# Seven quarter products instead of eight in the second layer of a fused attention and maxout kernel

## The chip, the cores and the metric

The kernel runs on one core of a Trainium2 chip. The time is the device time of one launch in microseconds; the figure before is the median of three runs, 149.65 us (149.41 to 149.71). A profile is a record of one execution; its span runs from the first instruction to the last.

## The reference

For each of 8 batches and 8 heads, 512 tokens x (64 wide) read from 32 state rows, and the state rows read from the tokens, both by softmax attention. The heads are put side by side (512 wide), and a two-branch layer with a maximum follows:

```python
xread = softmax(scale * x @ state.T) @ state          # 512 rows of each batch
sread = softmax(scale * state @ x.T) @ x              # 32 rows of each batch
x = concat([xread, sread]) -> (8 * 544, 512)
h1, h2 = x @ w1, x @ w2                               # 512 -> 1024
out = maximum(h1, h2) @ w_out                         # 1024 -> 512
```

## The kernel before

**Arithmetic.** The matmuls take bf16 and sum in float32 in PSUM, which has eight banks of 128 x 512 floats. The maximum is written h2 + relu(h1 - h2). So wd holds w1 - w2, and wwo holds the product w2 w_out; the output is xread wwo + relu(xread wd) w_out. The attention of the tokens is folded into the weights too: for a batch, sw_s holds, for the 256 state rows of all heads in two groups of 128, their products with wd (columns 0 to FF = 1024) and with wwo (columns FF to WC = 1536). With at_s, the transposed attention weights (256 state rows by 512 tokens), the first layer is r = relu(at_s x sw_s), transposed, 8 tiles of 128 features by 512 tokens (r_s, `l1_mm`, two matmuls a tile, evicted by `l1_ev` on ScalarE and VectorE in turn). The second layer, `l2(b, c)`, makes one chunk of 128 tokens by 512 columns in one bank: two opening matmuls (`l2_open`, at_s by the wwo part of sw_s) and eight (`l2_f`, a 128-feature tile of r by the 512 columns of wo). `l2_out` copies the bank into an output buffer, on VectorE for even chunks and on ScalarE for odd ones.

**Order.** Each engine runs its instructions in the order in which the program issues them; semaphores order the engines among each other. A list of tokens written out by hand (`ORDER`) gives the weights' loading and batches 0 and 1, with the attention of batch 2. A loop over b = 2 to 6 then does, with n = b + 1: the casts and the DMA transpose of x of batch b + 2 (`cast_b` on GpSimd, `xt_dma`), the first layer of b, the scores of n (`sc_mm`) with their exponential on ScalarE (`sc_ev`), the sums over state rows and their reciprocals on VectorE (`red`), the product of both on GpSimd (`mul`), the DMA transpose to at_s (`at_dma`), the casts of x of b + 2 (`cast_e`, GpSimd), the load of x of b + 3, and then the four chunks of the second layer of b. Between chunks 1 and 2 stand sw of n (`sw_mm`, three pieces of two banks each, six copies by VectorE and ScalarE in turn) and sr of n (`sr_mm`, the state rows' reading, evicted by `sr_ev` on VectorE, transposed by `sr_tr` and copied by `sr_cp`). In the turns b = 2 and 3, `sr_ev` and `sr_tr` of batches 0 and 1 stand in the loop too, from a buffer in SBUF. Last comes the store of batch b. A part of its own after the loop does batch 7 with the state rows' rows (`m1`, `m2`) and stores in pieces.

**Banks.** `bank(ring)` deals out the banks of a ring in turn: ring "r" has six, for the first layer, scores, sw and transposes; ring "a" has two, for the second layer's chunks and sr. A matmul that opens a bank waits until the last copy out of it is done.

**Buffers.** Ten buffers `big` of 128 x 2048 floats hold the loaded x, the weights as loaded and the outputs, dealt out in rotation.

Of the kernel before, what the change touches and what calls it, by code (L numbers as in the profile page):

```python
# [41 lines left out]
l2.0.0.o@6 sc.2.0@1 l2.0.3.1@3 exp.2.0>A l2.1.1.3@0 l2.0.2.o@2 red.2.0>V l2.1.3.1@4 l2.1.3.0@4 srp.0>P srp.1>P  # L42
# [9 lines left out]
WHOLE = ()  # L52
# [5 lines left out]
def kernel(  # L58
# [40 lines left out]
    def copy(eng, o, i):  # L99
        if eng == "A":  # L100
            nc.scalar.copy(o, i)  # L101
        elif eng == "V":
            nc.vector.tensor_copy(o, i)  # L103
        else:
            nc.gpsimd.tensor_copy(o, i)  # L105
# [37 lines left out]


    slot = {}
    for k, key in enumerate(["x0", "w20", "w10", "wo0", "w21", "w11", "wo1", "x1", "x2", "x3", "o0", "x4", "o1", "x5",
                             "o2", "x6", "o3", "x7", "o4", "o5", "o6", "o7"]):
        slot[key] = big[k % 10]

    def xf(b):  # L150
        return slot[f"x{b}"].rearrange("p (h m) -> p h m", h=H)
# [1 line left out]
    def ob(b):  # L153
        return slot[f"o{b}"].rearrange("p (c n) -> p c n", c=NC)
# [217 lines left out]
    def l1_ev(p, b, f, eng=None):  # L372
        relu(r_s[b % 2][:, f, :], p, eng)
# [11 lines left out]
    def l2_out(b, c, p, eng, lo=0, hi=DM):  # L385
        copy(eng, ob(b)[:, c, lo:hi], p[:, lo:hi])

    def l2(b, c, eng=None, ring="a"):
# [2 lines left out]
        l2_f(b, c, p, range(NF), False, True)  # L391
        l2_out(b, c, p, eng or ("A" if c % 2 else "V"))

    def store(b, c0=0, c1=NC, lo=0, hi=DM, eng=None):
        dst = out[b * L:b * L + S].rearrange("(p c) n -> p c n", c=NC)
        (eng or nc.sync).dma_start(out=dst[:, c0:c1, lo:hi], in_=ob(b)[:, c0:c1, lo:hi])
# [114 lines left out]
    def sw_range(b, z):  # L511
# [13 lines left out]
        idle=idle, fill=lambda k, r: idle(1, r, 512 if k >= 100 else 256, k >= 200), cS=s_cast, mS=lambda z, e: s_mask(z, LATE, B, e), Sd=lambda: s_dma(LATE, B), ce=cast_e, cb=cast_b, xtd=xt_dma,  # L525
        atd=at_dma, red=lambda b, h, e: red(b, h), mul=mul, cw2=w2_cast, sub=w_sub, cwo=wo_cast, ww=ww_mm, l2=l2_mm,
        wwe=lambda i, e: copy(e, wwo[:, i, :], open_[f"ww{i}"]), le=lambda b, c, e: l2_out(b, c, open_[f"l2{b}{c}"], e),
        Se=lambda lo, hi, j, e: s_ev(done[f"S.{lo}.{hi}"], lo, hi, j, e), store=store,
        swe=lambda b, z, g, e: sw_ev(done[f"sw.{b}.{z}"], b, *sw_range(b, z), g, e))
    done = {}  # L530
# [84 lines left out]

    for b in range(2, B - 1):
        n = b + 1
        if b + 2 < B:  # L620
            for g in range(2):
                cast_b(b + 2, g, "P")
            xt_dma(b + 2)
        for f in range(NF):
            l1_ev(l1_mm(b, f), b, f)
        pp = [sc_mm(n, hh) for hh in range(2)]
        for hh in range(2):
            sc_ev(pp[hh], n, hh)
        for hh in range(2):
            red(n, hh)  # L630
            mul(n, hh, "P")
        at_dma(n)
        if b + 2 < B:
            for k in range(4):
                cast_e(b + 2, k, "P")
        if b + 3 < B:
            if b + 3 in WHOLE:
                load_x(b + 3, 0, n=H)
            else:
                for g in range(2):  # L640
                    load_x(b + 3, g)
# [30 lines left out]
    l2(b, 0)  # L672
    l2(b, 1)
    store(b, 0, 2)
    tc.mark_branch_hint_location("gen", "LikelyTaken", [ENG.PE, ENG.Activation, ENG.DVE, ENG.Pool, ENG.SP])
    m2(0, "V")
    m_store(0)
    m2(1, "A")
    m_store(1)
    l2(b, 2, "V")  # L680
    store(b, 2, 3)
    for z, (lo, hi) in enumerate(((0, 256), (256, 512))):
        p = bank("a")
        l2_open(b, 3, p, True, False, lo, hi)
        l2_f(b, 3, p, range(NF), False, True, lo, hi)
        l2_out(b, 3, p, "VA"[z], lo, hi)
        store(b, 3, 4, lo, hi)
# [35 lines left out]
```

## Time and profile before

| | |
|---|---|
| median of three runs | 149.65 us |
| the profiled execution: span from first to last instruction | 147.7 us |
| outside the span, against the median | 1.95 us |
| TensorE busy | 139.9 us (95%) |
| VectorE, ScalarE, GpSimd busy | 84.6 us (57%), 70.3 us (48%), 49.5 us (34%) |
| granted TensorE clock, mean | 0.997 |
| moved by DMA | 29.44 MB |

In the profile PE is TensorE, PEld its weight loads, DVE is VectorE, ACT is ScalarE, POOL is GpSimd and SP is SyncE, which issues the DMAs; a name ending in q is an engine's instruction queue. A group's line gives the source line, the engine, the operation, what it writes and reads, the shapes, the count, the busy time in us and the mean of one in ns, and then the idle time before it with what ended it. A timeline's line gives start and duration in us and how many instructions are merged in it. Matmuls overlap in the pipeline, so that the time between their starts, not their length, tells their pace. Many lines are those of helpers: L101, L103 and L105 are the copies on ScalarE, VectorE and GpSimd, whatever is copied; the names of the operands tell which.

### The profile page before, as it was taken

The numbers are of one execution on the slowest core, as the hardware profiler recorded it, in microseconds if no ns is written. First come the engines' busy times: TensorE is split into PE (matmuls) and PEld (weight loads), VectorE is DVE, ScalarE is ACT, GpSimd is POOL, SyncE is SP. The second block draws the span as 40 slices with busy tenths as digits, with TensorE's granted clock in tenths as the row PEclk, the third lists the DMA queues.
The fourth block names the chain that finished last, engine by engine and source line by source line (L and its number), as shares of the span: only waits on it lengthen the run. The fifth ranks groups of instructions, "written<-read, shape, count | busy, mean of one in ns | idle before, by whom it ended". The sixth has DMA issues, their size and how long they took to land.

```text
span 147.7 us, 3018 instructions
## 1 busy us (share of the span) xinstructions
PE 139.9 (95%) x1176; PEld 70.9 (48%) x1194; DVE 84.6 (57%) x162; ACT 70.3 (48%) x129; POOL 49.5 (34%) x85
## 2 busy tenths in 40 slices
PE   6988999999999999999999999999999999999990
PEld 3566725444454445444544444454445444854460
DVE  3488868773324838863884576275738586630130
ACT  4358789898031766246441835281546236511100
POOL 4156320295039900912590447227400500000000
PEclk9999999999999999999999999999999999999998
DMA  4999999939990759979989785787306033302232
GB/s 133 323 346 398 384 389 381 319 63 176 260 344 18 135 114 391 266 126 383 192 172 276 263 182 100 255 296 134 71 36 249 16 62 142 142 4 105 108 142 80
DMA packets 35807, 29.44 MB, mean 199 GB/s; under 512 B 22608, under 2 KB 31312, under 8 KB 34896
## 3 DMA queue, kind: packets, MB, share of 16 engines
q1 hardware_dynamic: 35520, 29.10, 67.4%
q8 instruction: 10, 0.16, 0.5%
q10 hardware_dynamic: 272, 0.13, 0.3%
q14 instruction: 5, 0.04, 0.1%
HBM read 15.20 MB, written 8.91 MB: 163 GB/s over the span
## 4 chain that ended last, share of the span: by engine, by line
PE 83%; DMA 11%; ACT 1%; issue 1%; DVE 0%; SPq 0%; DVEq 0%
PE bank L382 38%; PE bank L368 19%; PE bank L377 9%; DMA big<-in_moe_w_out_dram 8%; PE bank L345 4%; DMA big<-in_x_dram 3%; PE bank L502 3%; PE bank L401 2%; PE bank L411 2%; PE bank L257 2%; PE bank L297 1%; PE bank L409 1%; ACT wo L101 1%; PE bank L441 1%; DVE sw L103 0%
## 5 line engine op out<-in xcount | busy, mean ns | idle before, releaser
L382 PE MATMUL bank<-wo,r 128*128 128x512 bf16 (+1 forms) x259 | 60.6, 372 | 0.6 <-issue 0.2
L382 PEld LDWEIGHTS <-r 128*128 128x128 bf16 x264 | 25.5, 98 | 28.9 <-issue 0.5
L363 DVE TENSOR_SCALAR r<-bank 128x512 bf16<-128x512 f32 x32 | 21.8, 690 | 18.2 <-PE bank L368 17.7
L101 ACT COPY big<-bank 128x512 f32<-128x512 f32 (+1 forms) x16 | 9.2, 573 | 44.4 <-PE bank L382 39.7
L368 PE MATMUL bank<-at,sw 128*128 128x512 bf16 x127 | 29.7, 379 | 0.2 <-DVE sw L103 0.2
L273 POOL TENSOR_TENSOR a<-e,er 128x512 bf16<-128x512 bf16 x14 | 14.5, 1050 | 33.0 <-DVE er L270 23.4
L361 ACT ACTIVATE r<-bank 128x512 bf16<-128x512 f32 x32 | 19.4, 612 | 5.1 <-PE bank L368 4.8
L105 POOL CAST xb<-big 128x1024 bf16<-128x1024 f32 x12 | 12.4, 1043 | 21.5 <-issue 13.0
L368 PEld LDWEIGHTS <-sw 128*128 128x128 bf16 x128 | 12.2, 98 | 14.5 <-ACT sw L101 0.5
L103 DVE COPY big<-bank 128x512 f32<-128x512 f32 (+1 forms) x17 | 11.2, 661 | 13.0 <-PE bank L382 13.0
L103 DVE CAST sw<-bank 128x512 bf16<-128x512 f32 x23 | 14.5, 683 | 6.7 <-PE bank L345 6.7
L105 POOL CAST xe<-big 128x512 bf16<-128x512 f32 x27 | 16.1, 632 | 5.9 <-DMA big<-in_x_dram 5.9
L377 PE MATMUL bank<-sw,at 128*128 128x512 bf16 (+1 forms) x56 | 16.8, 372 | 0.3
L269 DVE TENSOR_REDUCE sums<-e 128x16 f32<-128x512 bf16 x16 | 10.7, 666 | 6.2 <-ACT e L265 6.2
L101 ACT CAST sw<-bank 128x512 bf16<-128x512 f32 x25 | 13.1, 600 | 1.4 <-PE bank L345 1.4
L265 ACT ACTIVATE e<-bank 128x512 bf16<-128x512 f32 x16 | 9.0, 595 | 6.3 <-PE bank L257 5.7
L468 PE MATMUL bank<-wz 128*128 128x256 bf16 (+1 forms) x26 | 7.2, 428 | 1.3 <-DVE ones L471 1.3
L377 PEld LDWEIGHTS <-at 128*128 128x128 bf16 x66 | 5.6, 98 | 5.0
L502 PE MATMUL bank<-wo,w2m 128*128 128x512 bf16 x31 | 7.7, 379 | 0.2 <-ACT wo L101 0.2
L257 PEld LDWEIGHTS <-xt 128*128 128x128 bf16 x128 | 5.1, 98 | 2.6 <-DVE sbd L103 0.7
L257 PE MATMUL bank<-sbd,xt 128*128 128x64 bf16 x128 | 5.5, 193 | 0.5 <-DVE sbd L103 0.5
L103 DVE COPY w2m<-bank 128x1024 bf16<-128x1024 bf16 (+1 forms) x5 | 3.3, 687 | 4.3 <-PE bank L411 4.1
(71 smaller groups left out, 111.5 us busy)
## 6 DMA issues: line engine op xcount, KB each, us to landing
big<-in_x_dram SPq DMA_DIRECT2D x16, 512.0 KB, 5.3
out_dram<-big SPq DMA_DIRECT2D x7, 1024.0 KB, 4.2
big<-in_moe_w_dram SPq DMA_DIRECT2D x8, 512.0 KB, 11.8
big<-in_moe_w_out_dram SPq DMA_DIRECT2D x4, 512.0 KB, 11.5
out_dram<-big SPq DMA_DIRECT2D x1, 512.0 KB, 2.6
out_dram<-w2m SPq DMA_DIRECT2D x2, 256.0 KB, 2.4
sf<-in_state_dram SPq DMA_DIRECT2D x1, 384.0 KB, 10.4
out_dram<-big SPq DMA_DIRECT2D x1, 256.0 KB, 2.7
```

The source lines that it names most:

```text
L101: nc.scalar.copy(o, i)
L103: nc.vector.tensor_copy(o, i)
L105: nc.gpsimd.tensor_copy(o, i)
L257: nc.tensor.matmul(pv[:, c, kk], xt_s[b % 2][:, c, k, :], sbd[:, b, k, :], start=(c == 0 and kk == 0), stop=(c == NC - 1 and kk == 1))
L269: nc.vector.tensor_reduce(es_all[:, b, hh], e_view(e_s[b % 2], hh), axis=AXX, op=ALU.add)
L273: (nc.gpsimd if eng == "P" else nc.vector).tensor_mul(e_view(a_s[b % 2], hh), e_view(e_s[b % 2], hh), er_s[b % 2][:, hh].unsqueeze(3).to_b ...
L361: nc.scalar.activation(out=o, in_=p, func=ACTF.Relu)
L363: nc.vector.tensor_scalar(o, p, scalar1=0.0, scalar2=None, op0=ALU.max)
L368: nc.tensor.matmul(p, sw_s[b % 3][:, g, f * 128:(f + 1) * 128], at_s[b % 3][:, g].rearrange("p c t -> p (c t)"), start=(g == 0), stop=(g = ...
L377: nc.tensor.matmul(p[:, lo:hi], at_s[b % 3][:, g, c, :], sw_s[b % 3][:, g, FF + lo:FF + hi], start=(start and g == 0), stop=(stop and g == 1))
L382: nc.tensor.matmul(p[:, lo:hi], r_s[b % 2][:, f, c * 128:(c + 1) * 128], wo[:, f, lo:hi], start=(start and j == 0), stop=(stop and j == le ...
L502: nc.tensor.matmul(p, w2t[:, f, i, :], wo[:, f, :], start=(first and f % 2 == 0), stop=(last and f % 2 == 1))
```

## The change

For batches 2 to 7 the second layer's product r wo (512 tokens by 1024 features by 512 columns) is cut into two by two by two quarters: tokens i, features j, columns k (`rq(b, i, j)`, `wq(j, k)`). By one level of Strassen's algorithm in Winograd's form the four output quarters come from seven products of quarters. Each product is 2 groups of 128 tokens by 4 feature tiles, 256 columns wide: eight matmuls.

- Sums of r quarters go into `st` (four for each batch: `r_sum` 0, 1 and 3 on VectorE, 2 on GpSimd), sums of wo quarters into `wt` (four in all, GpSimd, `w_sum`). All are bf16, 128 x 1024.
- Three fixed banks, BX, BY and BZ, hold the partial sums. Where a later product adds on top of an earlier partial sum, the bank stays, and `keep` copies the partial sum into `part` (float32 in SBUF) on ScalarE before. `put` writes an output quarter: on VectorE as the bank plus a kept sum, the last one as a ScalarE copy.
- The opening terms are added to three quarters in the bank (`opened`); the last quarter inherits the opening of another column half and gets the difference (`difference`, GpSimd, into `dif`).
- Ring "r" has five banks, the sixth is BZ, which sw's last piece also uses. sr takes its bank from ring "r" and no longer from "a". Of the six sw copies VectorE does two and ScalarE four.
- The buffers under `wt`, `st`, `part` and `dif` are those of the loaded wo halves and of half of w1, free by then; x5 to x7 and the outputs change to others (`HOME`).
- For batch 7, the seven products are interleaved with `m2`, and the first half's store is issued after the sixth product, right before the last two stores.

```diff
-l2.0.0.o@6 sc.2.0@1 ... red.2.0>V l2.1.3.1@4 l2.1.3.0@4 srp.0>P srp.1>P
+l2.0.0.o@6 sc.2.0@1 ... red.2.0>V l2.1.3.1@4 l2.1.3.0@4 srp.0>P srp.1>P wt.0>P wt.2>P wt.1>P
...
-    rings = {"r": RELEASE[0:6], "a": RELEASE[6:8]}
+    rings = {"r": RELEASE[0:5], "a": RELEASE[6:8]}
+    BZ, BX, BY = RELEASE[5:8]
...
+    def add(eng, o, i0, i1, op=ALU.add):
+        (nc.gpsimd if eng == "P" else nc.vector).tensor_tensor(o, i0, i1, op=op)
+    def wq(j, k):
+        return wo[:, 4 * j:4 * j + 4, 256 * k:256 * k + 256]
+    def rq(b, i, j):
+        return r_s[b % 2][:, 4 * j:4 * j + 4, 256 * i:256 * i + 256]
+    def w_sum(k, eng):
+        a, c = ((wq(0, 1), wq(0, 0)), (wq(1, 1), wt[:, 0]), (wq(1, 1), wq(0, 1)), (wq(1, 0), wt[:, 1]))[k]
+        add(eng, wt[:, k], a, c, ALU.subtract)
+    def r_sum(b, k, eng):
+        a, c, op = ((rq(b, 1, 0), rq(b, 1, 1), ALU.add), (st[:, 0], rq(b, 0, 0), ALU.subtract),
+                    (rq(b, 0, 0), rq(b, 1, 0), ALU.subtract), (rq(b, 0, 1), st[:, 1], ALU.subtract))[k]
+        add(eng, st[:, k], a, c, op)
+    def difference(b, eng):
+        s3 = sw_s[b % 3]
+        add(eng, dif[:, b % 2], s3[:, :, FF:FF + 256], s3[:, :, FF + 256:WC], ALU.subtract)
+    def product(pv, lhs, rhs, first=False, cc=(0, 1)):
+        for c in cc:
+            for f in range(4):
+                nc.tensor.matmul(pv[c], lhs[:, f, 128 * c:128 * c + 128], rhs[:, f, :],
+                                 start=first and f == 0 and (c == 0 or pv.split), stop=False, skip_group_check=True)
+    def opened(b, pv, i, rhs, cc=(0, 1)):
+        for c in cc:
+            for g in range(2):
+                nc.tensor.matmul(pv[c], at_s[b % 3][:, g, 2 * i + c, :], rhs[:, g, :], start=False, stop=False,
+                                 skip_group_check=True)
...
+    w_sum(3, "P")
+    difference(2, "P")
     for b in range(2, B - 1):
...
         for f in range(NF):
             l1_ev(l1_mm(b, f), b, f)
+        r_sum(b, 2, "P")
+        pX, pY, pZ = Pair(BX), Pair(BY), Pair(BZ)
+        product(pX, rq(b, 0, 0), wq(0, 0), True)
+        keep(0, pX, "A")
         pp = [sc_mm(n, hh) for hh in range(2)]
         for hh in range(2):
             sc_ev(pp[hh], n, hh)
+        r_sum(b, 0, "V")
+        r_sum(b, 1, "V")
+        product(pZ, rq(b, 0, 1), wq(1, 0), True)
+        opened(b, pZ, 0, so_half(b, 0))
         for hh in range(2):
             red(n, hh)
             mul(n, hh, "P")
...
-        l2(b, 0)
+        put(b, 0, 0, pZ, 0)
+        product(pX, st[:, 1], wt[:, 1])
+        keep(1, pX, "A")
+        product(pY, st[:, 0], wt[:, 0], True)
+        keep(2, pY, "A")
+        r_sum(b, 3, "V")
         if b < 4:
             sr_ev(srd[:, b - 2], b - 2)
-        l2(b, 1)
-        pg = [sw_mm(n, 512 * z, 512 * z + 512) for z in range(3)]
-        p = sr_mm(n, "a")
+        pg = [sw_mm(n, 512 * z, 512 * z + 512, "r", BZ if z == 2 else "r") for z in range(3)]
         for z in range(3):
             for g in range(2):
-                sw_ev(pg[z], n, 512 * z, 512 * z + 512, g, "VA"[(z + g) % 2])
+                sw_ev(pg[z], n, 512 * z, 512 * z + 512, g, "VAA"[(z + 2 * g) % 3])
+        difference(n, "P")
+        product(pX, st[:, 2], wt[:, 2])
+        opened(b, pX, 1, so_half(b, 1))
+        p = sr_mm(n, "r")
+        put(b, 1, 1, pX, 2)
         sr_ev(p, n)
-        l2(b, 2)
...
-        l2(b, 3)
+        product(pY, st[:, 3], wq(1, 1))
+        opened(b, pY, 0, so_half(b, 1))
+        put(b, 0, 1, pY, 1)
         sr_cp(sr_tr(n, "r"), n, "A")
+        product(pX, rq(b, 1, 1), wt[:, 3])
+        opened(b, pX, 1, dif[:, b % 2])
+        put(b, 1, 0, pX, None, "A")
```

More of the change, by code (lines that the diff above doesn't have):

```diff
@@ new lines, in opened, with __init__, __getitem__ @@
+    def opened(b, pv, i, rhs, cc=(0, 1)):
[3 more added lines that the diff above has]
+                                 skip_group_check=True)
+    class Pair:
+        def __init__(self, lo, hi=None):
+            self.split = hi is not None
+            self.p = [bank(lo)] + ([bank(hi)] if self.split else [])
+        def __getitem__(self, c):
+            return self.p[c][:, 0:256] if self.split else self.p[0][:, 256 * c:256 * c + 256]
@@ new lines, in out_q, with keep, put @@
+    def out_q(b, i, k):
+        return ob(b)[:, 2 * i:2 * i + 2, 256 * k:256 * k + 256]
+    def keep(k, pv, eng):
+        if pv.split:
+            for c in range(2):
+                copy(eng[c], part[:, k, 256 * c:256 * c + 256], pv[c])
+        else:
+            copy(eng, part[:, k], pv.p[0])
+    def put(b, i, k, pv, kept=None, eng="V"):
+        for c in ((0, 1) if pv.split else (None,)):
+            o = out_q(b, i, k) if c is None else out_q(b, i, k)[:, c]
+            p = pv.p[0].rearrange("p (c n) -> p c n", c=2) if c is None else pv[c]
+            if kept is None:
+                copy(eng, o, p)
+            else:
+                u = part[:, kept].rearrange("p (c n) -> p c n", c=2)
+                add("V", o, p, u if c is None else u[:, c])
@@ L671 @@
     fv = nc.values_load(flag[0:1, 0:1], skip_runtime_bounds_check_because="compared with zero alone")
-    l2(b, 0)
-    l2(b, 1)
-    store(b, 0, 2)
[L675 to L687, printed above, removed]
+    r_sum(b, 2, "P")
+    r_sum(b, 0, "V")
+    r_sum(b, 1, "V")
+    r_sum(b, 3, "V")
+    pX, pY, pZ = Pair(BX, "r"), Pair(BY), Pair(BZ)
+    product(pX, rq(b, 0, 0), wq(0, 0), True)
+    keep(0, pX, "AV")
+    product(pZ, rq(b, 0, 1), wq(1, 0), True)
+    opened(b, pZ, 0, so_half(b, 0))
+    put(b, 0, 0, pZ, 0)
+    product(pX, st[:, 1], wt[:, 1])
+    keep(1, pX, "AV")
+    product(pY, st[:, 0], wt[:, 0], True)
+    keep(2, pY, "A")
+    tc.mark_branch_hint_location("gen", "LikelyTaken", [ENG.PE, ENG.Activation, ENG.DVE, ENG.Pool, ENG.SP])
+    m2(0, "V", "r")
+    m_store(0)
+    product(pX, st[:, 2], wt[:, 2])
+    opened(b, pX, 1, so_half(b, 1))
+    put(b, 1, 1, pX, 2)
+    store(b, 2, 4, 256, 512)
+    m2(1, "A", "r")
+    m_store(1)
+    product(pY, st[:, 3], wq(1, 1))
+    opened(b, pY, 0, so_half(b, 1))
+    put(b, 0, 1, pY, 1)
+    store(b, 0, 2)
+    for c in range(2):
+        product(pX, rq(b, 1, 1), wt[:, 3], cc=(c,))
+        opened(b, pX, 1, dif[:, b % 2], cc=(c,))
+        copy("VA"[c], out_q(b, 1, 0)[:, c], pX[c])
+        store(b, 2 + c, 3 + c, 0, 256)
     with tc.If(fv >= 1, preferred_fallthrough_block=True, label="gen"):
```

24 lines of the change are left out of this document (15 added, 9 removed).

## The prediction

> **What bounds the kernel now.** I read the page first (busy shares, chain), then TensorE's waits, its timeline over one batch, and then the queues of the engines that the change loads.
>
> ```profile
> span 147.7 us, 3018 instructions
> PE 139.9 (95%) x1176; PEld 70.9 (48%) x1194; DVE 84.6 (57%) x162; ACT 70.3 (48%) x129; POOL 49.5 (34%) x85
> PE 83%; DMA 11%; ACT 1%; issue 1%; DVE 0%; SPq 0%; DVEq 0%
> ...
> PE bank L468 <- DVE ones L471: 1.3, 1, 1.3
> PE bank L257 <- DVE sbd L103: 0.5, 1, 0.5
> ```
>
> TensorE is busy 95% of the span and is 83% of the chain that ended last. Its longest wait, 1.3 us, is at the very start and the next is 0.5 us, so in the main part it never waits: a matmul column taken away is time taken away, as long as nothing new makes TensorE wait. VectorE at 57% and GpSimd at 34% look free; that is where the change puts its additions. One batch (the turn with b = 4, on TensorE):
>
> ```profile
> 81.16 3.62 PE L368 MATMUL bank<-at,sw 128*128 128x512 bf16 x16
> 84.61 0.63 PE L257 MATMUL bank<-sbd,xt 128*128 128x64 bf16 x16
> 85.30 0.38 PE L377 MATMUL bank<-sw,at 128*128 128x512 bf16 x1
> ...
> 89.49 0.63 PE L345 MATMUL bank<-wd,sbd 64*32 64x512 bf16 x16
> ...
> 90.26 0.43 PE L297 MATMUL bank<-xe,e 128*32 128x65 bf16 x32
> 90.63 0.39 PE L377 MATMUL bank<-sw,at 128*128 128x512 bf16 x1
> ...
> 95.01 3.62 PE L368 MATMUL bank<-at,sw 128*128 128x512 bf16 x16
> ```
>
> Starts count, not durations, since matmuls overlap. A turn is 95.01 - 81.16 = 13.85 us. The first layer is 16 matmuls in 84.61 - 81.16 = 3.45, so 0.216 each for 512 columns. sw takes 0.77 (89.49 to 90.26), sr 0.37; the scores come to 0.47 (0.69 to the row at 85.30, of which 0.216 is a record of L377 that is missing: x1 stands where two are issued).
>
> **What the products save.** A chunk of the second layer is 2 + 8 matmuls of 512, a batch 40, or 40 x 0.216 = 8.64 us. Seven products are 7 x 8 matmuls of 256 columns, and the opening terms 16 more. The pace of 256 columns with a weight load each stands in the last chunk of today's kernel:
>
> ```profile
> 141.33 0.38 PE L377 MATMUL bank<-sw,at 128*128 128x256 bf16 x2
> 141.55 1.04 PE L382 MATMUL bank<-wo,r 128*128 128x256 bf16 x8
> 142.42 0.38 PE L377 MATMUL bank<-sw,at 128*128 128x256 bf16 x2
> ```
>
> Ten matmuls in 1.09 us, 0.109 each, so weight loads don't hold them. 72 x 0.109 = 7.85: 0.79 us less per batch, 4.74 us over six batches, if TensorE never waits.
>
> **What is added, and its price.**
>
> ```profile
> L103 DVE COPY big<-bank 128x512 f32<-128x512 f32 x16 | 10.8, 676 | 12.5 <-PE bank L382 12.5
> L103 DVE COPY big<-bank 128x256 f32<-128x256 f32 x1 | 0.4, 426 | 0.5 <-PE bank L382 0.5
> L103 DVE COPY w2m<-bank 128x1024 bf16<-128x1024 bf16 x4 | 2.6, 686 | 0.3 <-PE bank L441 0.2
> L101 ACT COPY big<-bank 128x512 f32<-128x512 f32 x15 | 8.8, 586 | 40.6 <-PE bank L382 35.9 <-PE bank L377 3.2 <-DMA big<-in_x_dram 1.5
> L273 POOL TENSOR_TENSOR a<-e,er 128x512 bf16<-128x512 bf16 x14 | 14.5, 1050 | 33.0 <-DVE er L270 23.4 <-ACT e L265 9.6
> L105 POOL CAST xe<-big 128x512 bf16<-128x512 f32 x27 | 16.1, 632 | 5.9 <-DMA big<-in_x_dram 5.9
> L105 POOL CAST xb<-big 128x1024 bf16<-128x1024 f32 x12 | 12.4, 1043 | 21.5 <-issue 13.0 <-DMA big<-in_x_dram 8.4
> ```
>
> - Sums of r, 1024 bf16 elements, three on VectorE. Between 0.69 us (the packed bf16 copy of 1024) and 1.19 (0.676 plus 512 elements at (676 - 426)/256 = 0.98 ns). I take 0.69: all three operands are packed bf16, like that copy's.
> - The fourth sum on GpSimd: between 1.05 (if packing helped) and 2.1 (twice the 512-element product). The casts give 0.80 ns an element and 0.22 fixed; the product's 0.83 over that fixed part, doubled, makes 1.9, which I take. The difference of the opening halves, 512 elements: 1.05.
> - put with an addend: a VectorE pass of 512 PSUM floats as in its copy, 0.69. keep and the last put: ScalarE copies at 0.59. ScalarE goes from two second-layer copies to four and takes four of six sw copies, not three: 3 x 0.59 more in 13.85, in its own gaps (35.9 us idle before those copies).
> - Weight sums: three of 1.9 = 5.7 us on GpSimd ahead of the product of batch 2, the fourth with batch 2's difference ahead of the casts of batch 4, whose scores come a turn later.
>
> ```profile
> 33.00 2.62 POOL L105 COPY wz<-sw 32x130 f32<-32x130 f32 x8
> 43.07 1.05 POOL L273 TENSOR_TENSOR a<-e,er 128x512 bf16<-128x512 bf16 x1 [7.45 <-DVE er L270]
> ```
>
> GpSimd idles 7.45 us there, from 35.62: 5.7 fits, nothing is late; at 2.1 each it still fits. Without that cover it would be 5.7 us on the path. The changed homes of x and o cost nothing: each new owner comes batches after the old one's last reader.
>
> **The new waits.** In the queues of a turn:
>
> ```profile
> 82.40 1.04 POOL L105 CAST xb<-big 128x1024 bf16<-128x1024 f32 x1 [0.41 <-DMA big<-in_x_dram]
> 86.92 2.06 POOL L273 TENSOR_TENSOR a<-e,er 128x512 bf16<-128x512 bf16 x2 [3.47 <-DVE er L270]
> ...
> 83.09 0.69 DVE L363 TENSOR_SCALAR r<-bank 128x512 bf16<-128x512 f32 x1 [0.17 <-PE bank L368]
> 84.02 1.48 DVE L363 TENSOR_SCALAR r<-bank 128x512 bf16<-128x512 f32 x2 [0.25 <-PE bank L368]
> 85.74 0.69 DVE L269 TENSOR_REDUCE sums<-e 128x16 f32<-128x512 bf16 x1 [0.23 <-ACT e L265]
> 87.60 0.63 DVE L103 COPY big<-bank 128x512 f32<-128x512 f32 x1
> ...
> 76.38 1.16 SPq L160 DMA_DIRECT2D big<-in_x_dram  x2
> 89.00 1.23 SPq L278 DMA_TRANSPOSE at<-a  x1
> ...
> DMA to landing us min/median/max: 3.0/3.2/3.9
> ```
>
> I count from the first layer's start (81.16 = 0). VectorE ends its last relu at 4.34. Undisturbed it then sums st0 (4.27 to 4.96) and st1 (5.06 to 5.75; consecutive passes overlap by 0.07, dependent ones don't), runs the two reductions with reciprocals (1.86, from 85.74 to 87.60), put of the first quarter 7.6 to 8.3, st3 to 8.9, then its sw copies. TensorE: first product 3.45 to 4.32, scores 4.79, second product with opening 6.10, third (wants st1) 6.97, fourth 7.84, sw 8.61 (its last bank wants that put), fifth with opening 9.92, then sr. sr moved from the "a" ring into a ring of five, where its bank is the one of the turn's first sw piece: it now waits until VectorE has copied that piece, and the sixth and seventh product wait in TensorE's queue behind it. Undisturbed the copy ends at 9.5: in time. The transposed a lands 1.18 + 2.06 + 3.2 after the reduction's start at 5.75, at 12.2, before the next turn at about 13.85 - 0.79 = 13.06. So undisturbed, turns 4 to 6 cost nothing extra. In turns 2 and 3 VectorE also has the deferred sr evictions between st3 and the sw copies, and these show the disturbance on which I decide:
>
> ```profile
> 60.00 1.05 POOL L273 TENSOR_TENSOR a<-e,er 128x512 bf16<-128x512 bf16 x1
> 60.43 0.67 DVE L305 TENSOR_SCALAR sr<-wz,sums 128x64 bf16<-128x64 f32 x1
> 60.99 0.61 POOL L105 CAST xe<-big 128x512 bf16<-128x512 f32 x1
> 61.02 0.63 DVE L305 TENSOR_SCALAR sr<-wz,sums 128x64 bf16<-128x64 f32 x1
> ...
> L305 DVE TENSOR_SCALAR sr<-bank,sums 128x64 bf16<-128x64 f32 x12 | 2.9, 279 | 0.2
> ```
>
> From PSUM this instruction takes 0.28 us. From SBUF, beside GpSimd, it takes 0.67 and 0.63, and ends at 61.10 and 61.65, within 0.05 of the ends of the GpSimd instructions it ran beside (61.05, 61.60). It waited for one whole GpSimd instruction each time. Whether a sum of two SBUF tensors does so no row shows; a reduction, with one SBUF tensor, keeps its 0.6 to 0.7. The nearest row is this one, and I take the sums to wait like it. The Trainium skill, SBUF — State Buffer, section Who interferes with whom, states it as a rule: a Vector instruction with two SBUF inputs and a GpSimd one that reads SBUF exclude each other for a whole instruction. By that rule the sum is the forecast's, without it the first rival's.
>
> Walked with that wait, turn by turn:
> - Turn 2: GpSimd's sum runs 2.65 to 4.55 (r's first half is there at 83.78, or 2.62); st0 slips to 5.25, st1 to 6.0: no wait yet. The put ends at 8.5, sw waits 0.2. st3 waits out the second product on GpSimd, to 9.8; the deferred sr evictions wait for two casts, to 11.0; the sw copy ends at 11.65 and sr, wanted at 10.1, waits 1.6. The transposes behind lose 0.15. Turn 14.9: +1.05.
> - Turn 3: the load of batch 5 ends its cast at 3.5 (issue to second cast is 6.0, 76.38 to 82.40, and issue follows the a transpose, now later); GpSimd's sum 3.5 to 5.4, st0 to 6.1, st1 to 6.85: the third product waits 0.8, sw 0.25, sr 1.6, the rest 0.15. Turn 15.8: +1.95.
> - Turn 4: loads early again after the long turn, as turn 2 without the deferred evictions: 0.2, 0.35, 0.2. Turn 13.7: -0.15.
> - Turn 5: cast ends at 3.75, GpSimd's sum at 5.65, st1 at 7.1: 1.05, 0.25, 0.4, 0.2. Turn 14.85: +1.0.
> - Turn 6: no casts; as turn 4: -0.15.
> - Batch 7: GpSimd is idle when VectorE sums. -0.79; the first kept quarter's VectorE half stands behind three sums (0.35, between 0 and 0.7). The store of half the output, today far from the end, is now issued some 1 us before the last two:
>
> ```profile
> out_dram<-big SPq DMA_DIRECT2D x1, 512.0 KB, 2.6
> ...
> out_dram<-big SPq DMA_DIRECT2D x2, 128.0 KB, 2.9
> ```
>
> It moves until 1.6 us after the last one's issue, inside that one's 2.9; I add 0.2 (0 to 0.6). Together -0.24.
>
> Sum: 1.05 + 1.95 - 0.15 + 1.0 - 0.15 - 0.24 = +3.46 us. The profiled span is 147.7, the median of three runs 149.65; the 1.95 between them lies outside the span and stays: 151.2 and **153.1**. With GpSimd's sum at 1.05 most of the waits of turns 3 and 5 go (-2), with sums of 1.19 another 2 come: 151 to 155.
>
> **Rivals.**
> - *The sums pass GpSimd freely.* For it: the reduction isn't slowed beside GpSimd, and the disturbed row has one SBUF tensor, not two. Then turns 4 to 6 and batch 7 keep 3 x 0.79 + 0.24 = 2.6, and turns 2 and 3 lose 0.2 each (sr waits 0.9 behind the deferred evictions, which the rows show disturbed today): -2.2, **147.4**. This is the faster side; it decides as long as st1 is there by 6.1.
> - *The sums run an element a cycle, 1.19, free of GpSimd.* st1 at 6.8, the put to 9.3, st3 to 10.4: waits of 0.75, 0.2, 0.2, 0.2 in each of turns 2 to 6 and some 1.2 more in 2 and 3: 9.2 against 4.74, **154.2**. Against it: the packed copy.
> - *The a transpose becomes late.* It has 0.8 us of room undisturbed; a 1 us later reduction would cost 0.2 a turn, 1 us in all. It would add to either side and decides nothing alone.
>
> That the change doesn't save its columns I exclude: their pace is in today's trace.
>
> **How the numbers follow.** Forecast 0.5, free sums 0.34, slow sums 0.12, anything else 0.04. A twentieth of the forecast's chance lies below today's time. About 0.2% (0.3 us) is what a measurement of this kernel can tell from no change; little of any case lies inside it. Faster 0.36, same 0.04, slower 0.60. Range 146.8 to 155.0: from the free sums with a tail that costs nothing to the upper end of the forecast; the forecast alone is 151 to 155.
>
> **What would show it.** In the changed profile the VectorE sums into st would take well over 0.69 on average, ending with GpSimd instructions; TensorE's waits would name VectorE, above all before L297 (sr) and before the third product; turns 2 and 3 would be the longest and 4 and 6 the shortest. If the st sums take 0.7 beside a busy GpSimd, turns 4 to 6 come to about 13.06 and I am wrong on the sign; if they take 1.2 with GpSimd idle, the third case holds.

## The result: 155.36 us against 149.66, and the profile after

The changed kernel takes 155.36 us (median of four runs, 154.72 to 156.46), the kernel before 149.66 beside it: ratio 1.0393, 95% interval 1.0348 to 1.0438. The forecast was slower, 153.1, range 146.8 to 155.0. The sign and the mechanism came as forecast; the time lies 2.3 us above the forecast and 0.36 above the range.

The profiled execution is the slowest of the four (156.46; the others have spans of 152.9 to 153.9). Its page, opening and chain:

```profile
span 154.7 us, 3478 instructions
...
PE 138.6 (90%) x1364; PEld 88.1 (57%) x1376; DVE 104.9 (68%) x184; ACT 79.8 (52%) x146; POOL 79.3 (51%) x101
...
PE 61%; DVE 19%; DMA 11%; ACT 2%; issue 2%; SPq 0%; DVEq 0%; ACTq 0%
```

VectorE now has 19% of the chain that ended last, where it had none. TensorE's waits in the main part name it:

```profile
PE bank L426 <- DVE big L402: 3.2, 3, 1.8
PE bank L304 <- DVE sw L104: 2.3, 2, 1.2
PE bank L426 <- DVE big L104: 0.4, 1, 0.4
```

L426 is `product`, L402 `add`, L304 `sr_mm`, L104 VectorE's copy. So three times (turns 3, 4 and 5) a product waited for a sum, and twice (turns 2 and 3) sr waited for the copy of sw; the last line is in batch 7, where a product waits for the copy of a kept quarter. The sums of r in the groups, one shape each (st0, st1 and st3 on VectorE, then st2 on GpSimd):

```profile
L402 DVE TENSOR_TENSOR big<-r 128x1024 bf16<-128x1024 bf16 x6 | 7.2, 1194 | 0.7 <-DVE w2m L370 0.2
L402 DVE TENSOR_TENSOR big<-big,r 128x1024 bf16<-128x1024 bf16 x6 | 5.9, 992 | 0.2
L402 DVE TENSOR_TENSOR big<-r,big 128x1024 bf16<-128x1024 bf16 x6 | 7.6, 1270 | 0.0
L402 POOL TENSOR_TENSOR big<-r 128x1024 bf16<-128x1024 bf16 x6 | 13.2, 2194 | 9.8 <-DVE r L370 9.8
```

A mean of 1.0 to 1.27 could be a slow instruction. That it is a wait is seen in the timelines of one turn (b = 5, start at 98.56), first VectorE, then GpSimd, then TensorE:

```profile
103.01 1.01 DVE L402 TENSOR_TENSOR big<-r 128x1024 bf16<-128x1024 bf16 x1
104.06 2.49 DVE L402 TENSOR_TENSOR big<-big,r 128x1024 bf16<-128x1024 bf16 x1
106.47 0.67 DVE L276 TENSOR_REDUCE sums<-e 128x16 f32<-128x512 bf16 x1
```

```profile
100.99 1.04 POOL L106 CAST xb<-big 128x1024 bf16<-128x1024 f32 x1 [2.99 <-DMA big<-in_x_dram]
102.44 1.04 POOL L106 CAST xb<-big 128x1024 bf16<-128x1024 f32 x1 [0.41 <-ACT r L368]
103.44 2.56 POOL L402 TENSOR_TENSOR big<-r 128x1024 bf16<-128x1024 bf16 x1
```

```profile
104.23 0.60 PE L432 MATMUL bank<-sw,at 128*128 128x256 bf16 x4
106.61 1.92 PE L426 MATMUL bank<-big,big 128*128 128x256 bf16 x16 [1.78 <-DVE big L402]
```

st0 ends at 104.02, 0.54 after the cast of x (103.48); st1 at 106.55, 0.55 after GpSimd's own sum (106.00). Each VectorE sum ends just behind the GpSimd instruction that was under way, and the third product starts when st1 is there. GpSimd's sum starts behind two casts of x, the first of which had waited 2.99 us for its load.

The turns, from the starts of the first layer in TensorE's timeline (the last three columns are kernels of the next section):

| | before | forecast | after | no sums | early loads | combined |
|---|---|---|---|---|---|---|
| ahead of turn 2 | 53.36 | 53.36 | 53.99 | 53.30 | 53.15 | 53.73 |
| turn 2 | 13.90 | 14.9 | 14.68 | 13.24 | 14.68 | 13.75 |
| turn 3 | 13.90 | 15.8 | 15.37 | 13.35 | 14.83 | 13.86 |
| turn 4 | 13.85 | 13.7 | 14.52 | 13.47 | 13.76 | 13.53 |
| turn 5 | 13.85 | 14.85 | 15.49 | 13.19 | 13.69 | 13.45 |
| turn 6 | 13.87 | 13.7 | 14.09 | 13.21 | 14.09 | 13.82 |
| batch 7 to the end of the span | 24.97 | 24.73 | 26.56 | 25.74 | 26.6 | 24.86 |

The loop loses 4.8 (74.15 against 69.37), batch 7 loses 1.6, and 0.6 lies ahead of the loop. The last is no more than scatter: in executions of the variants below, which all share that part but for the place of some loads, it lies between 53.15 and 54.05.

### The profile page after: what moved, and what is told of

The parts are those of the page before. It is cut to its first block, busy times and chain, and to the rows that moved or that the text cites. A ratio compares the mean times of both kernels' runs of the same rounds, so it can differ in the third digit from the quotient of the medians.

```text
span 154.7 us, 3478 instructions
## 1 busy us (share of the span) xinstructions
PE 138.6 (90%) x1364; PEld 88.1 (57%) x1376; DVE 104.9 (68%) x184; ACT 79.8 (52%) x146; POOL 79.3 (51%) x101
## 4 chain that ended last, share of the span: by engine, by line
PE 61%; DVE 19%; DMA 11%; ACT 2%; issue 2%; SPq 0%; DVEq 0%; ACTq 0%
PE bank L375 18%; PE bank L426 13%; DVE big L402 11%; PE bank L389 9%; DMA big<-in_moe_w_out_dram 8%; PE bank L432 4%; DMA big<-in_x_dram 3%; PE bank L574 3%; DVE sw L104 2%; PE bank L352 2%; PE bank L473 2%; DVE sums L276 2%; PE bank L384 2%; PE bank L483 2%; DVE r L370 2%
## 5 line engine op out<-in xcount | busy, mean ns | idle before, releaser
L102 ACT COPY big<-bank 128x512 f32<-128x512 f32 (+1 forms) x28 | 15.8, 563 | 30.2 <-PE bank L426 18.1
L426 PEld LDWEIGHTS <-big 128*128 128x128 bf16 x192 | 17.5, 98 | 8.9 <-DVE big L402 4.7
L426 PE MATMUL bank<-big,big 128*128 128x256 bf16 x144 | 18.0, 273 | 3.6 <-DVE big L402 3.2
L402 POOL TENSOR_TENSOR big<-r 128x1024 bf16<-128x1024 bf16 x6 | 13.2, 2194 | 9.8 <-DVE r L370 9.8
L389 PE MATMUL bank<-wo,r 128*128 128x512 bf16 x61 | 15.2, 379 | 0.3 <-issue 0.2
L402 DVE TENSOR_TENSOR big<-bank,big 128x512 f32<-128x512 f32 (+1 forms) x19 | 12.1, 643 | 4.7 <-PE bank L432 4.5
L426 PEld LDWEIGHTS <-r 128*128 128x128 bf16 x144 | 13.5, 98 | 2.5
L426 PE MATMUL bank<-wo,r 128*128 128x256 bf16 x96 | 12.3, 273 | 0.0
L104 DVE CAST sw<-bank 128x512 bf16<-128x512 f32 x18 | 11.4, 679 | 0.6 <-PE bank L352 0.6
L432 PE MATMUL bank<-sw,at 128*128 128x256 bf16 x72 | 10.8, 273 | 0.0
L432 PEld LDWEIGHTS <-at 128*128 128x128 bf16 x96 | 9.4, 98 | 1.1
L389 PEld LDWEIGHTS <-r 128*128 128x128 bf16 x64 | 5.9, 98 | 6.9 <-issue 0.5
```

Of the source, the lines that this page charges most:

```text
L389: nc.tensor.matmul(p[:, lo:hi], r_s[b % 2][:, f, c * 128:(c + 1) * 128], wo[:, f, lo:hi], start=(start and j == 0), stop=(stop and j == le ...
L402: (nc.gpsimd if eng == "P" else nc.vector).tensor_tensor(o, i0, i1, op=op)
L426: nc.tensor.matmul(pv[c], lhs[:, f, 128 * c:128 * c + 128], rhs[:, f, :], start=first and f == 0 and (c == 0 or pv.split), stop=False, ski ...
L432: nc.tensor.matmul(pv[c], at_s[b % 3][:, g, 2 * i + c, :], rhs[:, g, :], start=False, stop=False, skip_group_check=True)
```

## The experiments

The theory: the sums of two tensors in SBUF (where the operands lie that are not in PSUM) wait for whole GpSimd instructions, TensorE waits for the sums, and batch 7 ends later for its stores. Rivals: the sums are slow by themselves; the seven products don't save their columns; what stands around the sums (casts, evictions of sr) makes the wait, not the sums.

**The cost by itself.** The kernel before, with idle stretches of its last batch used as a bench; one execution.

```diff
+    mic = big[4].bitcast(BF16)
+    mif = big[5][:, 0:16]
+    w_a, w_b = w2m[:, 0:1024], w2m[:, 1024:2048]
+    for i in range(3):
+        nc.gpsimd.tensor_tensor(mic[:, 0:1024], w_a, w_b, op=ALU.add)
+    def probe():
+        for i in range(2):
+            nc.vector.tensor_tensor(mic[:, 1024:2048], w_a, w_b, op=ALU.add)
+            nc.vector.tensor_reduce(mif, w_a[:, 0:512].rearrange("p (a c) -> p a c", a=16), ...)
+    probe()      # beside the three GpSimd additions
     ...
+    probe()      # again, GpSimd idle
```

> The kernel before, with idle stretches of its last batch used to measure the disputed cost by itself: GpSimd adds two tensors in SBUF (1024 bfloat16 each) three times, VectorE beside that twice does the same addition followed by a reduction of 512 bfloat16 from one tensor; then VectorE does the same again with GpSimd idle. Theory (a VectorE addition of two SBUF tensors cannot run while a GpSimd instruction with two SBUF tensors is running): an addition beside busy GpSimd takes 1.0 to 2.7, ending within 0.7 behind the end of the GpSimd instruction, and 0.69 with GpSimd idle, while the reduction takes the same in both places. Rival (the sums are slow by themselves, or slow from sharing bandwidth): the additions take about the same in both places, or all VectorE work, the reductions too, is slowed by one common factor beside GpSimd.

VectorE's timeline in both places, then GpSimd's three additions (each one's length in ns, and when the first and the last start):

```profile
130.72 2.50 DVE L679 TENSOR_TENSOR big<-w2m 128x1024 bf16<-128x1024 bf16 x1 [0.32 <-DVE w2m L363]
133.14 0.67 DVE L680 TENSOR_REDUCE big<-w2m 128x16 f32<-128x512 bf16 x1
133.74 2.01 DVE L679 TENSOR_TENSOR big<-w2m 128x1024 bf16<-128x1024 bf16 x1
135.66 0.67 DVE L680 TENSOR_REDUCE big<-w2m 128x16 f32<-128x512 bf16 x1
...
141.72 0.68 DVE L679 TENSOR_TENSOR big<-w2m 128x1024 bf16<-128x1024 bf16 x1
142.32 0.68 DVE L680 TENSOR_REDUCE big<-w2m 128x16 f32<-128x512 bf16 x1
```

```profile
L676 POOL TENSOR_TENSOR big<-w2m x3: 2117/2447/2448, 130.5 to 135.3; 128x1024 bf16<-128x1024 bf16 x3
```

The same addition takes 2.50 and 2.01 beside GpSimd and 0.68 without; the reduction, with one SBUF operand, 0.67 and 0.68. The first GpSimd addition runs from 130.55 to 132.67, and VectorE's ends at 133.22, 0.55 later. GpSimd pays as well: 2.12 for the first and 2.45 for the two that had a VectorE addition ahead of them. The rival of slow sums falls. The Trainium skill (SBUF — State Buffer, Who interferes with whom) states this as an exclusive lock between a Vector instruction with two SBUF inputs and a GpSimd one that reads SBUF; the trace agrees, with the numbers above.

**No sums.** All sums of r are left out, and the products take quarters of r in their place (part of the computation is missing).

```diff
-        r_sum(b, 2, "P")
...
-        product(pX, st[:, 1], wt[:, 1])
+        product(pX, rq(b, 1, 0), wt[:, 1])
```

> Leaves out all sums of r: the products take quarters of r themselves (other numbers, same matmuls, copies and puts). Theory (what the change loses in the loop it loses to these sums and to who waits behind them): no wait before the third product, no GpSimd sum; turns 4 to 6 take 13.0 to 13.2 us, turns 2 and 3 13.2 to 14.0 with the deferred sr evictions; the time falls to 149.5 to 150.5, that is 5 us below the changed kernel, the rest being the tail's stores. Rival (the bank ring, the ScalarE copies or the matmul pace cost by themselves): turns 4 to 6 stay above 13.6.

TensorE has no wait in the main part, and the turns are 13.19 to 13.47, 66.46 in all against 69.37 before. So the seven products save 0.4 to 0.7 of the 0.79 a turn that was worked out; the rival without saving falls. The loop of the change is 7.7 us longer than this one, and the waits listed for it (3.2 and 2.3) make 5.5 of that; the rest is in no listed wait: turn 6 loses 0.88 against this kernel without one. The median, 149.63 (ratio 0.9997, 0.9976 to 1.0018), does not show it: the profiled run's span is 145.5 and its time 149.53, 4.0 apart, and in all ten runs it is 3.8 to 4.3, where the other kernels have 1.7 to 2.0. What lies outside the span there is not known, so this kernel is read by its turns only.

**Loads at the head of the turn.** The load of x of batch b + 3 is issued ahead of the transposes of x.

```diff
         n = b + 1
+        if b + 3 < B:
+            for g in range(2):
+                load_x(b + 3, g)
         if b + 2 < B:
```

> Loads of batch b + 3 issued at the start of the turn instead of behind the a transpose. Theory (a sum of two SBUF tensors on VectorE waits for the GpSimd instruction that runs): the casts no longer wait for the load, GpSimd's sum runs from about 2.6 to 4.8 after the turn's start, and VectorE's second sum is free of it. TensorE's waits before the third product, 0.58, 0.81 and 1.78 us in turns 3 to 5, go to under 0.2 each; turns 3 to 5 come down to about 14.8, 13.7, 13.7; the time by 2.5 to 3.2 us, to about 152.5. Rival (the sums are slow by themselves, or VectorE is simply full): the sums into st keep their lengths of 1.0 to 2.5 us, the time stays within 0.5 us.

It takes 154.62 (ratio 1.0326, 1.0301 to 1.0352), where I expected about 152.5. The waits before the third product are gone, and turns 3 to 6 are 14.84, 13.77, 13.69 and 14.09. But turn 2 takes 16.43. TensorE's waits, and SyncE's queue there:

```profile
PE bank L304 <- DVE sw L104: 2.3, 2, 1.2
PE bank L375 <- DMA at<-a: 1.6, 1, 1.6
```

```profile
55.75 2.32 SPq L167 DMA_DIRECT2D big<-in_x_dram  x2
58.17 8.86 SPq L242 DMA_TRANSPOSE xt<-xb  x1
67.14 1.24 SPq L285 DMA_TRANSPOSE at<-a  x1
```

The loads stand ahead of the transpose of x in SyncE's queue, that one starts at 58.17 and is held there until 67.03 (in the change it stood there from 55.89 to 62.61), and the transpose of a behind it is issued only at 67.14; the first layer waits 1.6 us for it. What holds a transpose so long was not tried.

**Loads a turn earlier.** The hand-written order ends with the load of batch 5, and each turn loads b + 4 at the old place.

```diff
-... sr.2@0 le.0.0>V sw.2.0@3,7 xtd.3
+... sr.2@0 le.0.0>V sw.2.0@3,7 xtd.3 ldx.5.0 ldx.5.1
...
-        if b + 3 < B:
+        if b + 4 < B:
             for g in range(2):
-                load_x(b + 3, g)
+                load_x(b + 4, g)
```

> Loads one turn earlier: x of batch 5 at the end of the hand-written order, x of b + 4 behind the a transpose in turn b. Nothing is put in front of the transposes, as it was with the loads at the start of the turn. Theory (the casts of x come late, push GpSimd's sum into VectorE's sums, and these exclude each other): the waits before the third product in turns 3 to 5 (0.58, 0.81, 1.78 us) go to under 0.2, turn 2 stays at about 14.7, turn 3 at 14.8 (its wait before sr of 1.1 stays), turns 4 and 5 at 13.7 to 13.8; the time falls by 2.5 to 3.2 us, to about 152.5. Rival (VectorE alone is too slow with three sums): less than 0.7 us.

152.9 us (ratio 1.0217, 1.0187 to 1.0247), 2.5 below the change. Waits and sums:

```profile
PE bank L304 <- DVE sw L104: 2.3, 2, 1.2
PE bank L426 <- DVE big L104: 0.4, 1, 0.4
```

```profile
L402 DVE TENSOR_TENSOR big<-r,big 128x1024 bf16<-128x1024 bf16 x6 | 7.6, 1269 | 0.0
L402 DVE TENSOR_TENSOR big<-r 128x1024 bf16<-128x1024 bf16 x6 | 5.9, 976 | 0.7 <-DVE w2m L370 0.2
L402 DVE TENSOR_TENSOR big<-big,r 128x1024 bf16<-128x1024 bf16 x6 | 4.2, 692 | 0.2
```

With the casts on time, GpSimd's sum runs beside the last relu and st0, and st1 takes 0.69 where it took 0.99; no product waits for a sum in the loop. What is left of the loss in the loop stands in turns 2 and 3, before sr.

**GpSimd's sum to VectorE.** All four sums on VectorE, st2 right ahead of st3.

```diff
-        r_sum(b, 2, "P")
...
         keep(2, pY, "A")
+        r_sum(b, 2, "V")
         r_sum(b, 3, "V")
```

> GpSimd's sum of r is moved to VectorE, in front of its third sum, in turns 2 to 6; one more sum on the loaded engine, none on GpSimd. Theory (exclusion): the first two sums on VectorE take 0.7 to 1.2 us (only a late cast is in their way) and the waits before the third product go to under 0.5 us in turns 3 to 5; the moved sum and the third wait for GpSimd's products instead, so the wait before sr grows by 0.6 to 1.3 us a turn. In all 1 us faster to 2 us slower than the changed kernel. Rival (VectorE's load is what costs): the waits before the third product stay and the time grows by 3 us or more.

155.7 (ratio 1.041, 1.0369 to 1.0451): no better. st0 and st1 are at 0.69 now, beside an idle GpSimd, but the moved sum and st3 run beside the products of scores (1.35 and 1.09 in one turn) and the fifth product waits for them in each turn:

```profile
PE bank L426 <- DVE big L402: 4.1, 5, 0.8
PE bank L304 <- DVE sw L104: 2.4, 2, 1.2
```

So it isn't one unlucky pair: whichever sum stands beside GpSimd's work pays.

**Deferred evictions later.** In turns 2 and 3 the evictions of sr from SBUF are moved from ahead of sw to behind the third put.

```diff
-        if b < 4:
-            sr_ev(srd[:, b - 2], b - 2)
...
         put(b, 0, 1, pY, 1)
+        if b < 4:
+            sr_ev(srd[:, b - 2], b - 2)
         sr_cp(sr_tr(n, "r"), n, "A")
```

> In turns 2 and 3 the deferred sr evictions of batches 0 and 1 are moved on VectorE from before the sw copies to behind the third put. Theory (sr waits on TensorE for the bank of the first sw piece, which VectorE copies only behind the third sum and these evictions): the waits of 1.19 and 1.14 us before sr in turns 2 and 3 shrink to about 0.2 each as in the other turns, the time falls by 1.6 to 2.2 us. Rival (the sum alone delays the copy): the waits stay above 0.8.

155.57 (ratio 1.0389, 1.0363 to 1.0416). Turn 2 falls to 13.67 and turn 3 to 15.24, and no wait before sr is left, but the time comes back as waits before the third product, 4.7 us in three; turn 4 takes 17.11. It fits that a shorter turn leaves the next load less time to land; that was not taken apart further. In that turn, after a wait of 2.18 us that ended at 90.69, the windows show a granted clock of one half (a line gives the stretch, its length, the busy time and count of PE, PEld, VectorE, ScalarE and GpSimd, then the granted clock, the DMA share and GB/s):

```profile
92.00:93.50 1.50, 1.50 (x15) 0.76 (x20) 1.40 (x4) 0.52 (x2) 1.50 (x2) 0.50 0.00 0
93.50:95.00 1.50, 1.50 (x26) 0.46 (x11) 1.50 (x3) 1.50 (x4) 1.50 (x3) 0.50 0.01 1
```

The first two pieces of sw take 0.83 in it (93.23 to 94.06), where they take 0.44 at the full clock (122.15 to 122.59 in the change).

**Batch 7 as before.** The loop of the change, and behind it the eight quarter products, `m2` and stores of the kernel before.

```diff
-    r_sum(b, 2, "P")
-    ...
-        store(b, 2 + c, 3 + c, 0, 256)
+    l2(b, 0)
+    l2(b, 1)
+    store(b, 0, 2)
+    m2(0, "V")
+    ...
```

> Batch 7's second layer is done as before the change (four chunks, the old stores); batches 2 to 6 stay as changed. Theory (the tail gains nothing on TensorE, 20.7 us from the first layer to the last matmul against 20.8 before, and loses 1.6 us behind the last eviction by the order of its stores): the time falls by 1.4 to 1.8 us, to 153.6 to 154.0. Rival (the seven products save their 0.79 us in the tail too): it falls by under 0.9 us.

153.69 (ratio 1.0262, 1.0231 to 1.0294): 1.67 us less than the change. Batch 7 to the end of the span takes 24.89 where it took 26.56.

**Half the half-store earlier.** The first quarter of the half output is stored right after its put, so that 256 KB instead of 512 go out in front of the last two stores.

```diff
     put(b, 0, 0, pZ, 0)
+    store(b, 0, 2, 0, 256)
...
     put(b, 0, 1, pY, 1)
-    store(b, 0, 2)
+    store(b, 0, 2, 256, 512)
```

> Theory (the stores behind the last eviction set the end): in the changed kernel the last ScalarE copy ends at 149.45 and the span at 154.7, 5.25 us later, against 3.6 us before the change; the half-output store lands 3.6 us after issue and the two 128 KB stores behind it 4.3 against 2.9. With one half of that store issued already after the first put, only 256 KB stand ahead of the last two: the stretch from the last copy to the end comes down to 3.6 to 4.2 us, the time by 1.0 to 1.6 us, to about 154. Rival (the tail's loss is in TensorE's waits for the kept quarter, 0.75 us): the time stays within 0.3 us.

154.9 (ratio 1.0364, 1.0339 to 1.0388): 0.46 less than the change, under half of what I expected, and not clear of the scatter (runs of 154.19 to 155.42 against 154.72 to 156.46). ScalarE's last copy starts at 147.09 and the span ends 5.3 later, against 5.6 in the change (149.08 to 154.7) and 4.0 before (143.71 to 147.7).

**A first combination.** Early loads; two pieces of sw ahead of the third product; the deferred evictions behind the third put; in batch 7 st3 behind the first put, and the store split as above.

```diff
+        pg = [sw_mm(n, 512 * z, 512 * z + 512) for z in range(2)]
...
         product(pX, st[:, 1], wt[:, 1])
...
         put(b, 0, 1, pY, 1)
+        if b < 4:
+            sr_ev(srd[:, b - 2], b - 2)
         product(pX, rq(b, 1, 1), wt[:, 3])
```

> Same seven products, another order: loads one turn earlier; the first two sw pieces before the third product, their first two copies on ScalarE; the deferred sr evictions behind the third put and the transposes of sr behind the last product; in batch 7 the third sum behind the first put, and half of the half-output store issued there. Theory (what was lost is lost to waits of TensorE behind VectorE, by order alone): turns 2 to 6 take 13.1 to 13.5 us, the span's end comes 4.0 us after the last eviction, and the time is 147 to 149, below the kernel before the change. Rival (with three sums VectorE, or the four sums with GpSimd, are too slow whatever the order): turns stay above 13.85, and the time above 150.

152.5 (ratio 1.0179, 1.0148 to 1.021), far from what I expected. Turns 4 to 6 are 13.53, 13.45 and 13.82, but 2 and 3 still 15.19 and 15.34. TensorE's waits and VectorE's timeline:

```profile
PE bank L336 <- DVE sr L312: 3.1, 2, 1.6
```

```profile
67.09 2.02 DVE L312 TENSOR_SCALAR sr<-wz,sums 128x64 bf16<-128x64 f32 x2
```

L336 is the transpose of sr, which waits for its evictions (L312). The two deferred evictions take 2.02 beside two casts on GpSimd and end at 69.11, 0.04 behind the second cast (69.07); the two from PSUM take 0.47 in that turn. Moved, they wait out other GpSimd instructions. So a multiplication with one SBUF tensor waits too, which a reduction does not. The Trainium skill (SBUF — State Buffer, Who interferes with whom) says so: where its operands meet the conditions, tensor_scalar can enter a mode that takes both ports and contends with GpSimd, a reduction never contends; the trace agrees, with 2.02 for the two here and 0.67 and 0.68 for the reduction of the bench.

**The combination, evictions on ScalarE.** As the last one, but the deferred multiplications run on ScalarE, and batch 7 is as before.

```diff
+    def sr_ev_a(p, b):
+        nc.vector.reciprocal(rr_all[:, b], p[:, 0:130:129])
+        for g in range(2):
+            nc.scalar.mul(sr_s[b % 2][:, g, :], p[:, 1 + 64 * g:65 + 64 * g], rr_all[:, b, g:g + 1])
...
-            sr_ev(srd[:, b - 2], b - 2)
+            sr_ev_a(srd[:, b - 2], b - 2)
```

> Combination: the loads of a turn fetch the batch after the one they fetch now, the first two pieces of sw are computed ahead of the third product with their evictions on ScalarE, the multiplications of the two deferred evictions of sr are moved from VectorE to ScalarE, and batch 7 has eight quarter products as before. Theory (all of the loss in the loop is TensorE waiting for VectorE and GpSimd, behind casts that come late and behind evictions of sr that stand behind the sums): no wait is left in turns 2 to 6, so they take 13.4 to 13.6 each instead of 13.9, 67.5 in all against 69.4 before; with batch 7 as before the kernel takes 147.4 to 148.6, below before by 0.7 to 1.5 per cent. Rival (the sums of r on VectorE cost whatever GpSimd does, and the moved work only shifts the wait): turns 2 and 3 stay above 14.5, and the kernel stays between 149.6 and 152.

148.61 us (148.48 to 148.84), ratio to before 0.9925, 0.9905 to 0.9946: faster than both kernels. The page and the sums:

```profile
span 147.0 us, 3413 instructions
...
PE 138.5 (94%) x1341; PEld 85.5 (58%) x1354; DVE 93.8 (64%) x173; ACT 79.5 (54%) x148; POOL 76.5 (52%) x100
```

```profile
L407 DVE TENSOR_TENSOR big<-r,big 128x1024 bf16<-128x1024 bf16 x5 | 3.9, 771 | 0.0
L407 DVE TENSOR_TENSOR big<-big,r 128x1024 bf16<-128x1024 bf16 x5 | 3.5, 691 | 0.2
```

No wait of TensorE of 0.2 us or more is listed in the loop, and turns 2 and 3 are 13.75 and 13.86. The loop takes 68.41, 1.0 less than before. This is 2 us above the loop without sums: in turn 6, for one, the last piece of sw takes 0.73 where it takes 0.33 without sums (`wwo`, 116.92 to 117.65 against 114.94 to 115.27), which fits its bank BZ coming free only after the first put; that was not tried.

**The same loop, seven products in batch 7, stores ahead of `m2`.**

```diff
     put(b, 0, 1, pY, 1)
-    store(b, 0, 2)
+    store(b, 0, 2, 256, 512)
+    m2(0, "V", "r")
+    m_store(0)
+    m2(1, "A", "r")
+    m_store(1)
     for c in range(2):
         product(pX, rq(b, 1, 1), wt[:, 3], cc=(c,))
```

> The same loop, but batch 7 also by seven quarter products, six of them with their stores ahead of the two small products m2, and the last one behind these. Theory (what batch 7 lost in the changed kernel is the order of its stores and the two waits for its sums): last matmul 0.5 to 0.8 earlier than in the combination with the old batch 7, and with two thirds of the output stored before m2 the span ends no later than there, so 0 to 0.8 below it. Rival (the end is set by several small stores that land together behind the last copy, whatever goes ahead of them): the last copy ends earlier, but the end of the span lies 4.5 to 5.5 behind it instead of 3.6, and the kernel is 0.3 to 1.2 above the other.

148.66 (ratio 0.9939, 0.9919 to 0.9959): the same as the last one. ScalarE's last copy in this kernel, and in the combination:

```profile
142.10 0.37 ACT L102 COPY big<-bank 128x256 f32<-128x256 f32 x1 [0.72 <-PE bank L437]
```

```profile
143.13 0.37 ACT L102 COPY big<-bank 128x256 f32<-128x256 f32 x1 [3.76 <-PE bank L394]
```

From the start of batch 7 (121.77 and 122.14) that is 20.33 and 20.99: TensorE keeps its 0.66. The span ends 4.5 after the copy's start, not 3.9, so that 0.6 is given back. It is given back in SyncE's queue: the two last stores land in 2.4 us, quicker than before the change, but the first of them takes 1.13 us to issue (0.34 before), and the last is issued at 143.25, 0.78 behind the end of its copy (142.47).

## Why the prediction was right in kind and too low

**The mechanism held.** The step that decided, that sums of two SBUF tensors wait for whole GpSimd instructions, is shown by the bench and by turn 5. Its prices: 0.69 for a sum beside idle GpSimd, as taken; a put 0.67 and a keep 0.59, as taken; GpSimd's sum 2.12 undisturbed, the upper end of 1.05 to 2.1, not the 1.9 taken. The casts on GpSimd got slower too (688 ns on average against 632 before and 623 without the sums), which had no term.

**The loop's term was nearly right, in part by luck.** The forecast makes the five turns 72.95. Its turns follow from its waits only if a turn without waits takes 12.95, where the text itself works out 13.06 (13.85 less 0.79). From 13.06 the same waits give 15.01, 15.86, 13.81, 14.96 and 13.81, which is 73.45, and the time would have been 153.6. (The arithmetic for slow sums, too, gives 154.1, not 154.2.) The profiled execution has 74.15, but it is the slowest of four, and in two other executions of the same loop (half the half-store earlier, batch 7 as before) the sums are 72.98 and 73.38. That the total fits is luck in part, for the turns err both ways. Turns 2 and 3 were put a little high (14.9 and 15.8; 14.68 and 15.37), turns 5 and 6 too low (14.85 and 13.7; 15.49 and 14.09). Turn 4 is 14.52 in the profiled run and 13.77 and 13.76 in those two, against 13.7. What moves it is when the casts come, and that the walk took too rigidly, from one distance of 6.0 us between issue and second cast: here turns 4 and 5 wait 0.81 and 1.78 before the third product. With loads a turn earlier both waits go, and 2.5 us of the time.

**The step that failed is the store in batch 7.** The sum had 0.2 (0 to 0.6) for the half output going out right ahead of the last two stores. From the start of ScalarE's last copy to the end of the span, before has 4.0 and after 5.6: 1.6 us in its place.

```profile
143.71 0.37 ACT L101 COPY big<-bank 128x256 f32<-128x256 f32 x1 [3.76 <-PE bank L382]
```

```profile
149.08 0.37 ACT L102 COPY big<-bank 128x256 f32<-128x256 f32 x1 [2.04 <-PE bank L432]
```

The landing times of the stores around it, after:

```profile
out_dram<-big SPq DMA_DIRECT2D x1, 512.0 KB, 3.6
...
out_dram<-big SPq DMA_DIRECT2D x2, 128.0 KB, 4.3
```

The last ones land in 4.3, where they landed in 2.9. I had reckoned that the half store's 2.6 us lie inside that 2.9; they do not run beside each other for nothing, and `m_store`, now 1.4 us ahead of the half store, moves in the same stretch. In the same batch the saving of TensorE (0.79, less 0.35 of waits) came to 0.04: from the first layer's start to that copy 20.94 against 20.98. The third product waits 0.13 for st1, and its second half 0.62 for the kept quarter's copy, which stands behind the three sums on VectorE (both by the starts, at 0.109 a matmul; the row's 0.45 counts from the end of the matmul before):

```profile
138.46 1.47 PE L426 MATMUL bank<-big,big 128*128 128x256 bf16 x12 [0.45 <-DVE big L104]
```

So batch 7 costs +1.6 where -0.24 stood, and undoing batch 7 alone gives back 1.67. That is 1.8 of the 2.3 us that were missing; the other 0.5 has the size of what the walk lost by starting from 12.95, and lies within the loop's scatter.

What stays open is what in those stores costs the time. Halving the half store gave only 0.3 between copy and end, and nothing in the first combination, which has the same split (5.8); moving all output stores but the last two ahead of `m2` gave 1.1 of the 1.6 (4.5 from copy to end). In the change the last store is issued right behind its copy (149.47; the copy ends at 149.45), so the loss lies in that issue (0.70, where it took 0.33 before) and behind it, not ahead of it as in the kernel with the stores ahead of `m2`. Bytes in flight, the size of their packets and the closeness of `m_store` weren't told apart.

**The rivals.** That of sums free of GpSimd falls: it gave 13.06 for turns 4 to 6, which not even the kernel without sums reaches (13.2 to 13.5). But its condition, st1 in time for the third product, is what the combination brings about by other means, and that one is faster than before, by 1.1 us. That of slow sums (1.19) falls at 0.69. The late transpose came only where loads were put ahead of it.

## What to carry to other kernels

Idle time of VectorE and GpSimd wasn't free capacity here, where both read SBUF: before moving adds to VectorE, list which of its instructions have two SBUF operands, or multiply out of SBUF, and which GpSimd instructions lie beside them, and count a whole GpSimd instruction for each meeting. A saving on TensorE survives only if each new operand is there on time, so give the slack first (earlier loads, evictions on an engine that doesn't meet GpSimd), then the arithmetic. Price the end of a kernel apart: here the stores issued in the last few microseconds cost 1.6 us from the last copy to the end of the span, twice what TensorE could save in that batch.

## What the runs showed of the hardware

- The wait works both ways: GpSimd's addition goes from 2.12 to 2.45 when a VectorE one has come in between, and VectorE's ends 0.55 behind GpSimd's.
- A multiplication of 64 floats with a single SBUF tensor also waited on VectorE (two in 2.02, beside GpSimd), a reduction with a single SBUF tensor did not (0.67).
- After TensorE had waited 2.18 us its granted clock was 0.50 for some 3 us, from about 1 us behind the wait's end; it fell in the same way after a wait of 2.73 us in the bench (0.56 and 0.59 in the stretches 138 to 140 and 140 to 142; the wait ended at 136.99). After a wait of 1.78 us in the changed kernel it stayed at 1.00. So a wait can cost more than its length.
